# Sparse attention and a squared-ReLU expert in one kernel: batch 0 in query halves, expert chunk 0 in token halves, one-hot global rows, and casts per tile on VectorE and ScalarE

## The chip, the cores and the metric

The kernel runs on one core of one Trainium2 chip. The metric is the device time of one execution in microseconds (us), lower is better. A median is given with the number of runs behind it. Engine names: PE is TensorE, PEld its weight load, DVE is VectorE, ACT is ScalarE, POOL is GpSimd, SP is SyncE, which issues most DMA transfers here.

## The reference

Two operations follow each other. The first is attention in which a query sees a window of 32 positions on each side and 8 chosen "global" positions; global positions see and are seen by everything. The second is a two-matrix expert with a squared ReLU.

```python
# q, k, v: (8 batches, 8 heads, 576 positions, 64); global_idx: 8 sorted positions, known only at run time
scores = scale * np.matmul(q, k.transpose(0, 1, 3, 2))
mask = np.abs(pos[:, None] - pos[None, :]) <= 32
mask = mask | is_global[:, None] | is_global[None, :]
attn = softmax(np.where(mask, scores, -1e9))
x = (attn @ v) laid out as (4608 tokens, 512)
out = np.maximum(x @ w_in, 0) ** 2 @ w_out       # w_in: 512 x 2048, w_out: 2048 x 512
```

All inputs are float32; the kernel computes with 16-bit floats, so each batch of q, k and v must be cast after it is loaded.

## The kernel before

The 64 steps are (batch, head). Each step computes the scores of one head, the product with v of the head before, and four "fills" of expert work, so that TensorE always has something to do while ScalarE and VectorE handle the softmax. The expert works on 9 chunks of 512 tokens. For each chunk there are 16 "expert-in" fills (matmul with `w_in`, ReLU, square) and then 16 "expert-out" fills (matmul with `w_out`), so the work alternates between an expert-in half of four steps and an expert-out half of four steps. In the steady part, one chunk goes with one batch.

```python
def mm1(c, u):                                   # expert-in: 4 matmuls of 128x512
    ph = ps.tile([P, TC], FP32, name="ph", tag="m", bufs=3)
    ...                                          # cut: the 4 matmuls into ph
    rl = sbt("rl", [P, TC], FP16, bufs=3)
    nc.scalar.activation(out=rl, in_=ph, func=AF.Relu)
    nc.vector.tensor_tensor(out=gts[c][:, u, :], in0=rl, in1=rl, op=ALU.mult)

def tr_q(b, hp):                                 # transposes of q for two heads
    src = qnat[b % 2]
    for i in range(NT):                          # NT = 5 tiles of 120 (last: 96) positions
        nc.tensor.transpose(pt[:, ...], src[0:n, i, ts(hp, P)], identity[0:n, 0:n])
    ...                                          # cut: VectorE copies of pt into qa, qb

for s in range(B * H):
    b, h = divmod(s, H)
    n = b + 1
    if s == 1:
        ...                                      # cut: casts of batch 0, load of w_in, first fetch of batch 1
    if s == 6:
        nc.gpsimd.dma_start(out=w_out, in_=moe_w_out...)
    if h == 1 and 0 < b < B - 1:                 # next batch is cast on GpSimd, 120x2048 and 96x512 at a time
        cast(nc.gpsimd.tensor_copy, knat[n % 2], sts["k"])
        gload_kq(n)                              # 8 global rows of k and q, from a DRAM scratch
    if h == 2 and 0 < b < B - 1:
        cast(nc.gpsimd.tensor_copy, qnat[n % 2], sts["q"])
    if h == 4 and 0 < b < B - 1:
        cast(nc.gpsimd.tensor_copy, vx[n % 2], sts["v"], w=P)
        gload_v(n)
    if h == 5 and b + 2 < B and b > 0:
        fetch_next(n + 1)                        # 15 transfers, float32, into staging
    ...                                          # cut: gathers of global rows
    if s == H:                                   # expert chunk 0 runs here in one lump,
        ...                                      # cut: with the casts of batch 1 on GpSimd
    et = scores(b, h)                            # TensorE scores, ScalarE Exp -> er, VectorE mask -> et
    nb, nhp = divmod(s // 2 + 1, H // 2)
    if nb < B and s not in (H - 2, H - 1):
        (tr_q if h % 2 == 0 else tr_k)(nb, nhp)  # at h == 6 these are the NEXT batch's first q tiles
    fill(s, 2)
    if prev is not None:
        pv(*prev)                                # acc, Ln, Exp(-Ln), xT
    fill(s, 2)
    prev = (b, h, et)
```

The softmax here doesn't subtract the row's maximum and nothing guards it: scores larger than these inputs give would overflow.

## Time and profile before

The median is 402.03 us (3 runs, 398.62 to 402.93); the profiled execution spans 401.8 us at a mean granted clock of 0.983. There are three stretches.

| stretch (us) | what happens | what sets the time |
|---|---|---|
| 0 to 59.7 | loads, mask, batch 0 attention | DMA near 190 GB/s and one chain per head; no expert matmul |
| 59.7 to 117.9 | expert chunk 0 in a lump, batch 1 | mixed; loads of batch 2 and `w_out` under way |
| 117.9 to 401.8 | steady part, then a tail of expert work alone | TensorE |

Two lines of the page of before, from its part 1 (busy time of each engine and its share of the span) and part 2 (granted clock in 40 slices of the span, each about 10 us, in tenths of full speed):

```profile
PE 336.4 (84%) x2240; PEld 188.1 (47%) x2240; DVE 277.5 (69%) x603; ACT 225.3 (56%) x341; POOL 107.9 (27%) x169
PEclk9999999969979999999999999999999999999999
```

The clock is near full except for two slices in the start. The view is the chain of waits of before, in order of time (start, duration, engine and line). It shows a step at its undisturbed pace and then the one thing in each batch that disturbs it:

```profile
185.60 0.26 PE ptq L356 x5
185.86 1.73 PE po L322 x8
187.59 0.38 PE acc L403 x6
187.97 1.73 PE po L322 x8
189.70 0.38 PE sc L383 x6
...
194.83 1.74 PE ph L307 x8
196.58 0.02 issue
196.60 0.61 ACT rl L312
197.21 0.01 issue
197.22 4.70 DVE gt L313 x2
...
202.16 0.77 DVE xT L420
```

A step is 2.37 + 2.11 = 4.48 us of gapless TensorE work, so eight steps are 35.9 us. But the pattern repeats every 38.0 us (the `xT` at 164.17 comes again at 202.16). The missing 2.1 us lies in the last lines: two squares `gt` that take about 0.42 us each elsewhere take 4.70 us together. The timeline of before at that place (start, duration, engine, operation) says why:

```profile
196.60 2.44 POOL L105 CAST qnat_72<-stg 120x2048 f16<-120x2048 f32 x2
197.22 4.69 DVE L313 TENSOR_TENSOR gt<-rl 128x512 f16<-128x512 f16 x2
198.99 2.64 POOL L105 CAST vx_74<-stg 120x2048 f16<-120x2048 f32 x2
202.98 0.41 PE L403 MATMUL acc<-et,vx_73 128*128 128x160 f16 x4 [1.92 <-DVE xT L420]
```

VectorE's square stands still while GpSimd casts back to back, and TensorE is idle for 1.92 us behind it. The trace has five such places, once per batch.

The stretch table of before gives the engines' busy time in one period (columns: window, its length, then busy time of PE, PEld, DVE, ACT, POOL with instruction counts, granted clock, DMA share, GB/s):

```profile
164.17:202.16 37.99, 36.07 (x264) 20.67 (x264) 31.51 (x68) 26.20 (x41) 10.17 (x15) 1.00 0.76 124
```

### The profile page before, as it was taken

To read this page: it belongs to the slowest core of one execution; us is meant where nothing else is said; L and a number is where in the kernel's file an instruction comes from. 1 tells how busy PE (TensorE), PEld (TensorE's weight loads), DVE (VectorE), ACT (ScalarE), POOL (GpSimd) and SP (SyncE) were. 2 spreads that over 40 slices of the span, in tenths; PEclk is the share of its full clock that TensorE was granted. 3 is DMA by queue.
4 is the path that set the end of the run, shared out by engine and by line. 5 is a ranking of instruction groups with operands and counts; after the bars stand their busy time and mean duration, and the time that the engine had idled before them with its cause. 6 is when DMAs were issued, how large, how long until landed. Compare 5 with 4: busy or idle time off the path is not lost.

```text
span 401.8 us, 6380 instructions
## 1 busy us (share of the span) xinstructions
PE 336.4 (84%) x2240; PEld 188.1 (47%) x2240; DVE 277.5 (69%) x603; ACT 225.3 (56%) x341; POOL 107.9 (27%) x169
## 2 busy tenths in 40 slices
PE   0037529779768999899989989998999999999996
PEld 0025414445444555455545545554555554444442
DVE  3787636756789868986898689679867874432531
ACT  1126724634657956785597469656955982530620
POOL 5929427250048006200930180036001001000000
PEclk9999999969979999999999999999999999999999
DMA  8979998961999942991599189410001002001002
GB/s 149 192 119 190 201 194 173 197 121 62 182 198 171 186 102 82 180 160 54 121 166 153 49 164 191 90 59 34 2 33 74 1 2 78 29 8 71 28 26 78
DMA packets 126549, 43.86 MB, mean 109 GB/s; under 512 B 117110, under 2 KB 121590, under 8 KB 126518
## 3 DMA queue, kind: packets, MB, share of 16 engines
q1 hardware_dynamic: 117618, 38.29, 52.3%
q0 software_dynamic: 5904, 4.39, 7.0%
q10 hardware_dynamic: 2996, 0.79, 1.0%
q8 instruction: 17, 0.28, 0.3%
q14 instruction: 14, 0.11, 0.1%
HBM read 38.14 MB, written 9.70 MB: 119 GB/s over the span
## 4 chain that ended last, share of the span: by engine, by line
PE 72%; DVE 18%; ACT 5%; issue 2%; POOL 1%; DMA 1%; POOLq 0%; DVEq 0%
PE po L322 31%; PE ph L307 26%; DVE gt L313 6%; PE acc L403 6%; PE sc L383 5%; DVE xT L420 3%; DVE et L393 2%; PE ptq L356 2%; PE ptk L373 1%; ACT ln L415 1%; ACT ln L413 1%; ACT er L388 1%; DMA gp_100<-in_global_idx_dram 1%; ACT rl L312 1%; DVE knat_69 L105 1%
## 5 line engine op out<-in xcount | busy, mean ns | idle before, releaser
L307 PE MATMUL ph<-xT,w_in 128*128 128x512 f16 x576 | 136.2, 386 | 5.6 <-POOL xT L435 5.6
L322 PE MATMUL po<-w_out,gt 128*128 128x512 f16 x576 | 135.0, 383 | 0.0
L312 ACT ACTIVATE rl<-ph 128x512 f16<-128x512 f32 x144 | 83.7, 600 | 58.0 <-PE ph L307 44.4
L313 DVE TENSOR_TENSOR gt<-rl 128x512 f16<-128x512 f16 x144 | 81.9, 592 | 24.2 <-ACT rl L312 23.0
L307 PEld LDWEIGHTS <-w_in 128*128 128x128 f16 x576 | 55.0, 99 | 64.4 <-issue 10.1
L322 PEld LDWEIGHTS <-gt 128*128 128x128 f16 x576 | 54.4, 98 | 56.5 <-issue 1.7
L388 ACT ACTIVATE er<-sc 128x880 f16<-128x880 f32 x64 | 57.9, 905 | 31.1 <-PE sc L383 30.9
L413 ACT ACTIVATE ln<-acc 64x576 f32<-64x576 f32 x64 | 41.2, 645 | 54.6 <-PE acc L403 53.3
L435 POOL COPY xT<-gx 128x4 f16 x64 | 15.2, 238 | 203.7 <-DVE gx L431 200.2
L420 DVE TENSOR_TENSOR xT<-acc,ln 64x576 f16<-64x576 f32 x64 | 48.3, 754 | 22.5 <-ACT ln L415 22.1
L393 DVE TENSOR_TENSOR et<-er,mask 128x880 f16<-128x880 f16 x64 | 42.3, 662 | 15.0 <-ACT er L388 14.3
L415 ACT ACTIVATE ln<-ln 64x576 f32<-64x576 f32 x64 | 43.6, 681 | 2.0
L328 DVE COPY ot<-po 128x512 f32<-128x512 f32 x36 | 24.6, 685 | 24.7 <-PE po L322 24.1
L383 PEld LDWEIGHTS <-kT 128*128 128x128 f16 x384 | 30.4, 106 | 23.1 <-DVE kT L375 7.7
L373 PE MATMUL ptk<-identity,knat_69 128*128 128x128 f16 x80 | 8.4, 242 | 27.5 <-DVE knat_69 L105 19.8
L403 PE MATMUL acc<-et,vx_73 128*128 128x160 f16 (+2 forms) x192 | 20.3, 251 | 12.6 <-DVE xT L420 12.6
L416 DVE TENSOR_REDUCE gs<-acc 128x8 f32<-128x32 f32 x64 | 12.2, 191 | 21.4 <-ACT ln L413 20.1
L403 PEld LDWEIGHTS <-vx_73 128*128 128x128 f16 x192 | 15.8, 109 | 20.1 <-issue 7.8
L403 PE MATMUL acc<-et,vx_74 128*128 128x160 f16 (+2 forms) x192 | 18.0, 232 | 5.0 <-DVE xT L420 5.0
L403 PEld LDWEIGHTS <-vx_74 128*128 128x128 f16 x192 | 14.2, 100 | 12.9 <-DVE xT L420 4.8
L373 PEld LDWEIGHTS <-knat_69 128*128 128x128 f16 x80 | 5.6, 106 | 29.2 <-DVE knat_69 L105 20.0
L375 DVE COPY kT<-ptk 128x640 f16<-128x640 f16 x32 | 15.7, 489 | 1.0 <-PE ptk L373 0.4
(79 smaller groups left out, 248.4 us busy)
## 6 DMA issues: line engine op xcount, KB each, us to landing
out_dram<-ot SPq DMA_DIRECT2D x36, 256.0 KB, 2.1
stg<-in_k_dram SPq DMA_DIRECT2D x28, 240.0 KB, 5.0
stg<-in_q_dram SPq DMA_DIRECT2D x28, 240.0 KB, 11.7
stg<-in_v_dram SPq DMA_DIRECT2D x28, 240.0 KB, 6.1
w_in<-in_moe_w_in_dram POOLq DMA_DIRECT2D x4, 512.0 KB, 11.0
w_out<-in_moe_w_out_dram POOLq DMA_DIRECT2D x1, 2048.0 KB, 19.2
stg<-in_k_dram SPq DMA_DIRECT2D x7, 192.0 KB, 5.3
stg<-in_q_dram SPq DMA_DIRECT2D x7, 192.0 KB, 5.4
```

The source lines that it names most:

```text
L307: nc.tensor.matmul(ph, w_in[:, t, u * P : (u + 1) * P], xT[:, t, c * TC : (c + 1) * TC], start=(t == 0), stop=(t == NDM - 1),)
L312: nc.scalar.activation(out=rl, in_=ph, func=AF.Relu)
L313: nc.vector.tensor_tensor(out=gts[c][:, u, :], in0=rl, in1=rl, op=ALU.mult)
L322: nc.tensor.matmul(po, gts[c][:, f, m * P : (m + 1) * P], w_out[:, f, :], start=(f == 0), stop=(f == NFF - 1),)
L328: nc.vector.tensor_copy(out=ot, in_=po)
L383: nc.tensor.matmul(sc[:, bank, so : so + w], kT[:, ts(t, P)], qx[:, c0 : c0 + w], start=True, stop=True,)
L388: nc.scalar.activation(out=er.rearrange("p (b c) -> p b c", b=2), in_=sc[:, :, 0:SCW], func=AF.Exp, bias=0.0, scale=scale,)
L393: nc.vector.tensor_tensor(out=et, in0=er, in1=mask, op=ALU.mult)
L403: nc.tensor.matmul(acc[:, bank, o : o + w], vx[b % 2][:, t, v0 : v0 + P], et[:, base : base + w], start=(i % 3 == 0), stop=(i % 3 == 2), s ...
L413: nc.scalar.activation(out=ln[nr], in_=av[dr, :, :, 0:GTOK], func=AF.Ln)
L415: nc.scalar.activation(out=rec[nr], in_=ln[nr], func=AF.Exp, scale=-1.0)
L420: nc.vector.tensor_tensor(out=xT[nr, hp, b * S : (b + 1) * S].rearrange("p (b k x) -> p b k x", b=2, k=2), in0=av[nr, :, :, 0:GTOK], in1=r ...
```

## The change

The intent is to start expert work earlier and to take the casts away from GpSimd.

- Batch 0 attention runs in two query halves, and expert chunk 0 in two token halves, so that the first half chunk can start when the first queries are done.
- The 8 global rows of batch 0 are picked with one-hot matmuls instead of by an indirect DMA.
- The next batch's casts are 15 tile casts on VectorE and ScalarE, spread over heads 1 to 5. There is now a single staging set; as each tile is cast, the same tile of the batch after it is fetched.
- The global rows of batch 1 and later are fetched in float32 to the front of every staging tile, so that a tile's cast also covers them. These rows are fetched last, after all 15 tiles.
- The load of `w_out` is held back until batch 1's tiles have landed.

```diff
-    if h == 1 and 0 < b < B - 1:
-        cast(nc.gpsimd.tensor_copy, knat[n % 2], sts["k"])
-        gload_kq(n)
-    if h == 2 and 0 < b < B - 1:
-        cast(nc.gpsimd.tensor_copy, qnat[n % 2], sts["q"])
-    if h == 4 and 0 < b < B - 1:
-        cast(nc.gpsimd.tensor_copy, vx[n % 2], sts["v"], w=P)
-        gload_v(n)
-    if h == 5 and b + 2 < B and b > 0:
-        fetch_next(n + 1)
...
+def cast_batch(n, t):
+    cast_tile(nc.vector.tensor_copy, "k", n, t)
+    cast_tile(nc.scalar.copy, "q", n, t)
+    cast_tile(nc.vector.tensor_copy if t % 2 else nc.scalar.copy, "v", n, t)
...
+for h in range(H):                              # batch 0, first query half
+    et = scores(0, h, (0,))
+    ...                                         # cut: casts, transposes, v globals per pair of heads
+    if h == 5:
+        for nm in "kqv":
+            for t in range(NT):
+                fetch(nc.sync, nm, 1, t)
+        fetch_globals(1)
+    ...                                         # cut: memsets for batch 1, prev, step
+for h in range(H):                              # batch 0, second query half
+    et = scores(0, h, (1,))
+    fill(step, 1); pv(*prev); fill(step, 1)
+    ...                                         # cut: prev, step
+    if h == 1:
+        nc.gpsimd.tensor_copy(out=w_out[0:1, 0, 0:1], in_=st["v"][32:33, 4, 511:512])   # holds w_out back
+        for i in range(4):
+            nc.gpsimd.dma_start(out=w_out[:, ts(i, 4), :], in_=wo[:, ts(i, 4), :])
+    if h >= 5:
+        for t in ((0,), (1, 2), (3, 4))[h - 5]:
+            cast_batch(1, t)
...
+for b in range(1, B):
+    n = b + 1
+    plan = {3: (0, 1), 4: (2, 3), 5: (4,)} if b == 1 else {t + 1: (t,) for t in range(NT)}
+    for h in range(H):
+        if b == 1 and h == 0:
+            ...                                 # cut: fetch of all tiles of batch 2
+            fetch_globals(n)
+        et = scores(b, h, (0, 1))
+        nb, nhp = divmod(b * NHP + h // 2 + 1, NHP)
+        if nb < B:
+            (tr_q if h % 2 == 0 else tr_k)(nb, nhp)
+        fill(step, 2)
+        if prev is not None: pv(*prev)
+        fill(step, 2)
+        prev = (b, h, (0, 1), et)
+        for t in plan.get(h, ()) if n < B else ():
+            cast_batch(n, t)
+            if n + 1 < B:
+                for nm in "kqv":
+                    fetch(nc.sync, nm, n + 1, t)
+        ...                                     # cut: gathers of global rows
+        if h == 7 and n + 1 < B:
+            fetch_globals(n + 1)
```

`tr_q` now transposes its five tiles in reverse order, `for i in reversed(range(NT))`, so the first of them needs the tile that is cast last.

## The prediction

> **What bounds it now.** The page gives 401.8 us, TensorE 84% busy. The chain of waits has three stretches.
> (1) 0 to 59.7 us: no expert matmul. The first `et` is at 28.9 us: the mask waits for indices by DMA and a GpSimd memset. Then each head of batch 0 costs 3.1 us: accumulate 0.91, Ln 0.66, Exp 0.69, `xT` 0.77; one `acc`, so nothing overlaps. DMA runs near 190 GB/s.
> (2) 59.7 to 116.5 us: chunk 0 runs in one lump while GpSimd casts batch 1; four later steps hold only attention (about 3.3 us each).
> (3) From 116.5 us: TensorE bound. The chain repeats every 38.0 us per batch. An unhindered step is 2.37 + 2.11 = 4.48 us, 35.9 per batch; the other 2.1 us is one stall: in the timeline at 197.2 us two `gt` products take 4.69 us (median 0.425 each) while GpSimd casts `qnat` and `vx` (1.9 us each). The Trainium skill, "SBUF — State Buffer", section "SBUF: two separate sides", says VectorE and GpSimd share a port pair as an exclusive lock; this trace agrees. Five such stalls remain. The tail from 335.6 us is pure matmul at 0.216 us each and doesn't change.
>
> **Change.** Removed: GpSimd casts with their stalls (5 x 2.1 = 10 us); the index wait; the single `acc` of batch 0; the attention-only steps (chunk 0 is spread over the second half and batch 1). Added: one-hot matmuls, two evacuations per pair; per batch 8 ScalarE casts (about 0.6 us, interpolated between the traced 0.40 at 256 and 1.04 at 1024 elements) and 7 VectorE casts (about 0.6).
>
> *Steady part.* In the expert-in half ScalarE already fills 4.35 of 4.48 us per step (0.90+0.64+0.68+4x0.54), VectorE about 4.0. Casts at heads 1 to 5 land there and add about 3 us to each; buffers should hide most. I expect stalls of 1 us per batch instead of 2.1: gain 5 us.
>
> *Start.* First scores near 18 us, first half about 3 us per step (casts, transposes and copies in the same queues), ending near 43; expert matmuls from 47. But loads bind: batch 0 is issued until about 26 us, `w_in` takes about 13, batch 1 about 19, so batch 1 lands near 59; `w_out` and batch 2 near 90. In-order casts on ScalarE and VectorE wait for whole batches plus globals, which GpSimd used to absorb: about 5 us near 54 to 59, some 8 us at batch 1, head 3. So batch 2, head 2 (116.5 us before) comes at 110 to 121. Batch 2 can be fetched only after batch 1 is cast: one staging set. The early expert work is mostly given back to loads.
>
> Sum: 402 - 5 (steady) - 2 (start) = **395 us, range 379 to 409**. Chances: faster by over 2% 0.45, within 2% 0.47, slower 0.08.
>
> **What would show it.**
> - First expert matmul between 44 and 50 us, half width; first `et` by 20 us.
> - No `gt` above 1 us in the steady part; batch period 36.5 to 37.5 us.
> - Casts waiting for staging DMA in the second half of batch 0 and at batch 1 heads 3 to 5; TensorE idle there.
> - ScalarE near full in the expert-in half; `ph` waiting for ReLU or `acc` for `xT` about 1 us per batch.
> - Batch 2, head 2 within 5 us of 116.5.
>
> **What would make it wrong.** If batches 1 and 2 land before their casts are reached, the start gains 15 to 20 us and the time is 375 to 380. If casts stall TensorE 2 to 4 us per batch, the steady gain vanishes and it is 400 or more.

## The result, and the profile after

The median after is 426.69 us (5 runs, 424.65 to 429.4), against 402.03 us before (5 runs on the same chip, 398.4 to 402.93). The ratio is 1.0636, with a 95% interval of 1.0565 to 1.0707: slower. Here and below, a ratio is the mean time of one kernel's fast runs over that of the other's of the same rounds, so it isn't quite the ratio of the medians quoted. The range of the prediction (379 to 409) did not hold the result.

The same two lines of the page, after:

```profile
PE 350.9 (82%) x2402; PEld 203.1 (48%) x2402; DVE 268.9 (63%) x711; ACT 264.9 (62%) x453; POOL 45.8 (11%) x124
PEclk9999965785999989998999999899989999999999
```

GpSimd is relieved (107.9 to 45.8 us) and ScalarE took over (225.3 to 264.9). The clock line has new dips: a broad one in slices 6 to 10, and then single 8s, of which some are four slices apart, which is one batch.

A convenient mark is the first expert matmul at head 2 of a batch, where the steady pattern begins. Spans are those of the profiled executions. The profiled run of after is the slowest of its five (429.4 us, median 426.69), so a difference of up to 3 us between its profile and another run's can be that alone.

| mark | before (us) | after (us) | difference |
|---|---|---|---|
| first expert matmul | 59.7 | 44.2 | -15.5 |
| batch 2, head 2 | 117.9 | 131.0 | +13.1 |
| batch 6, head 2 | 270.8 | 293.6 | +22.8 |
| end of the span | 401.8 | 427.3 | +25.5 |

So the start loses 13.1 us although it begins 15.5 us earlier, and from there on the steady part loses the remaining 12.4.

**The steady part.** The chain of waits after reaches the mark at 171.71, 212.36, 252.99 and 293.63 us: a period of 40.65 us. The stretch table for one period, and for that of the next period cut into four:

```profile
171.71:212.36 40.65, 38.23 (x266) 21.28 (x264) 29.98 (x76) 30.16 (x49) 2.00 (x8) 0.96 0.64 120
...
212.36:230.81 18.45, 18.12 (x127) 9.99 (x125) 15.84 (x42) 17.81 (x31) 0.00 (x0) 1.00 0.85 148
230.81:233.34 2.53, 0.44 (x6) 0.39 (x7) 1.84 (x4) 2.51 (x6) 0.00 (x0) 1.00 1.08 186
233.34:237.10 3.76, 3.76 (x16) 1.82 (x14) 1.61 (x5) 0.83 (x2) 0.00 (x0) 0.55 0.93 166
237.10:253.00 15.90, 15.90 (x119) 9.27 (x118) 10.69 (x25) 9.01 (x13) 2.00 (x8) 1.00 0.25 66
```

In the first part, the expert-in half, ScalarE is busy for 17.81 of 18.45 us: ReLUs, softmax and casts fill its queue. In the second part TensorE does almost nothing and the clock is still 1.00. In the third, TensorE works without a pause, but at a granted clock of 0.55 on average: it is 0.50 for 3.41 us of it, from 233.62 to 237.03 us. In the last part everything is back to normal and ScalarE has time to spare (9.01 of 15.90). The timeline of TensorE after, then that of ScalarE, across that gap (in brackets: the idle time before, and what ended it):

```profile
230.26 0.55 PE L451 MATMUL sc<-qa_80,kT 128*128 128x160 f16 x6
232.90 0.45 PE L390 MATMUL tr<-identity,qnat_71 104*128 104x104 f16 x5 [2.09 <-ACT qnat_71 L309]
233.18 3.18 PE L345 MATMUL mm<-w_out,gt 128*128 128x512 f16 x8
```

```profile
228.77 1.08 ACT L333 ACTIVATE rl<-mm 128x512 f16<-128x512 f32 x2
...
231.25 1.09 ACT L333 ACTIVATE rl<-mm 128x512 f16<-128x512 f32 x2
232.22 0.62 ACT L309 CAST qnat_71<-stq 104x512 f16<-104x512 f32 x1
```

TensorE reaches head 6 and finds that the last q tile of the next batch isn't cast. The cast is at the end of a ScalarE queue that has never paused. As the transposes go in reverse order, all five wait, and with them the expert-out matmuls that are ready behind them. After the gap the first group of eight expert-out matmuls takes 3.18 us by the timeline, where the same group takes 1.89 us later. The five slow `gt` squares of before are gone: the longest `gt` of after takes 0.43 us.

**The start.** The waits of TensorE after, from 40 to 110 us (in all, how often, the longest), then those of ScalarE from 50 to 108 us:

```profile
PE mm L328 <- ACT rl L333: 14.2, 3, 13.1
PE acc L478 <- DVE et L466: 12.7, 2, 10.5
PE mm L328 <- POOL xT L521: 7.0, 2, 3.6
```

```profile
ACT qnat_70 L309 <- DMA stq<-gscr_q_362: 11.5, 1, 11.5
ACT qnat_71 L309 <- DMA stq<-gscr_q_301: 9.0, 1, 9.0
```

The third line of the first fence is GpSimd's copy of global columns into `xT`; it belongs to the halves themselves (a run without these loads, e6 below, has the same 7.0 us). The first two lines hold two long gaps of TensorE, of 10.45 us up to 64.6 us and of 13.06 us up to 104.5 us. In each, ScalarE and VectorE stand before the first cast of a batch and wait for the transfer named `gscr`: the global rows, fetched behind all 15 tiles of the batch. The first cast of batch 1 could start at 61.6 us, that of batch 2 at 101.1 us, and the first q casts 0.6 to 0.9 us later. In the stretch table the granted clock is 0.50 from 56.1 to 80.0 us, although TensorE works again from 64.6 us, with pauses.

### The profile page after: what moved, and what is told of

It is laid out like the page before. It is cut to its first block, busy times and chain, and to the rows that moved or that the text cites. A ratio compares the mean times of both kernels' runs of the same rounds, so it can differ in the third digit from the quotient of the medians.

```text
span 427.3 us, 6931 instructions
## 1 busy us (share of the span) xinstructions
PE 350.9 (82%) x2402; PEld 203.1 (48%) x2402; DVE 268.9 (63%) x711; ACT 264.9 (62%) x453; POOL 45.8 (11%) x124
## 4 chain that ended last, share of the span: by engine, by line
PE 53%; ACT 15%; issue 12%; DVE 4%; SPq 2%; DMA 1%; POOL 1%; ACTq 0%; POOLq 0%
PE mm L345 30%; PE mm L328 14%; ACT rl L333 6%; PE acc L478 3%; PE sc L451 3%; ACT er L465 3%; ACT ln L490 2%; PE tr L390 2%; DMA stq<-gscr_q_362 1%; SPq L121 1%; ACT qnat_70 L309 1%; DVE et L466 1%; ACT qnat_71 L309 1%; PE tr L415 1%; POOL w_out L597 1%
## 5 line engine op out<-in xcount | busy, mean ns | idle before, releaser
L328 PE MATMUL mm<-xT,w_in 128*128 128x512 f16 (+1 forms) x640 | 143.8, 367 | 22.9 <-ACT rl L333 15.9
L345 PE MATMUL mm<-w_out,gt 128*128 128x512 f16 x576 | 140.5, 394 | 0.0
L333 ACT ACTIVATE rl<-mm 128x512 f16<-128x512 f32 (+1 forms) x160 | 83.8, 554 | 40.6 <-PE mm L328 38.6
L465 ACT ACTIVATE er<-sc 128x880 f16<-128x880 f32 (+2 forms) x72 | 59.4, 825 | 21.6 <-PE sc L451 21.2
L334 DVE TENSOR_TENSOR gt<-rl 128x512 f16<-128x512 f16 (+1 forms) x160 | 59.4, 394 | 20.3 <-ACT rl L333 15.8
L490 ACT ACTIVATE ln<-acc 64x576 f32<-64x576 f32 (+1 forms) x72 | 42.6, 592 | 46.5 <-PE acc L478 45.4
L498 DVE TENSOR_TENSOR xT<-acc,ln 64x576 f16<-64x576 f32 (+1 forms) x72 | 49.6, 689 | 30.1 <-ACT ln L491 27.1
L466 DVE TENSOR_TENSOR et<-er,mask 128x880 f16<-128x880 f16 (+2 forms) x72 | 40.5, 562 | 29.1 <-ACT er L465 26.3
L491 ACT ACTIVATE ln<-ln 64x576 f32<-64x576 f32 (+1 forms) x72 | 45.2, 628 | 2.3
L351 DVE COPY ot<-mm 128x512 f32<-128x512 f32 x36 | 24.7, 685 | 24.9 <-PE mm L345 24.4
```

Source lines behind the costliest of these rows:

```text
L328: nc.tensor.matmul(ph, w_in[:, t, u * P : (u + 1) * P], xT[:, t, c * TC + a : c * TC + z], start=(t == 0), stop=(t == NDM - 1),)
L333: nc.scalar.activation(out=rl[:, 0 : z - a], in_=ph, func=AF.Relu)
L334: nc.vector.tensor_tensor(out=gts[c][:, u, a:z], in0=rl[:, 0 : z - a], in1=rl[:, 0 : z - a], op=ALU.mult)
L345: nc.tensor.matmul(po, gts[c][:, f, m * P : (m + 1) * P], w_out[:, f, :], start=(f == 0), stop=(f == NFF - 1),)
L465: nc.scalar.activation(out=ev, in_=sv, func=AF.Exp, bias=0.0, scale=scale)
L466: nc.vector.tensor_tensor(out=tv, in0=ev, in1=mv, op=ALU.mult)
```

## The experiments

All ran beside the kernel before on the same chip; its median in those rounds was 400.46 to 401.59 us. Each experiment has 4 runs. "Head 2" means the first expert matmul of batch 2, head 2 (after: 131.0 us), and "period" the repeat of the steady pattern (after: 40.65 us).

| run | change | median us | ratio to before (95%) | head 2 | period |
|---|---|---|---|---|---|
| e1_pool_casts | after, casts on GpSimd | 412.56 | 1.0264 (1.0204 to 1.0325) | 131.1 | 36.16 |
| e2_late_tr | after, transposes of head 6 later | 411.16 | 1.0270 (1.0238 to 1.0302) | 128.6 | 37.43 |
| e3_casts_out_half | after, casts at heads 0, 1 | 412.22 | 1.0296 (1.0263 to 1.0329) | 131.7 | 36.44 |
| e4_no_load2 | after, batch 2 not loaded (wrong result) | 418.70 | 1.0451 (1.0401 to 1.0500) | 121.9 | 40.6, once 39.0 |
| e5_wout_early | after, `w_out` not held back | 429.89 | 1.0686 (1.0642 to 1.0731) | 135.0 | 40.6, once 39.0 |
| e6_no_load12 | after, batches 1 and 2 not loaded (wrong result) | 407.78 | 1.0129 (1.0075 to 1.0183) | 112.0 | 40.6 |
| e7_before_casts_out | before, tile casts at heads 0, 1 | 396.24 | 0.9861 (0.9799 to 0.9923) | | 36.73 |
| e8_before_casts_in | before, tile casts at heads 1 to 5 | 443.34 | none (two of four runs slow) | | about 47 |
| e8b_before_casts_in | the same, fetches per tile | 405.43 | 1.0124 (1.0072 to 1.0177) | | 38.69 |
| e9_dummy_mm | after, the gap filled with dummy matmuls | 422.47 | 1.0527 (1.0477 to 1.0576) | 134.3 | 38.94 |
| e10_casts_lump | after, casts of batches 1, 2 in one lump | 425.27 | 1.0593 (1.0540 to 1.0646) | about 127.5 | |
| e11_lump_out_late | e10, e3 and e2 together | 409.32 | 1.0191 (1.0135 to 1.0247) | 129.9 | 36.44 |
| e12_globals_mid | after, global rows fetched between k and q | 422.78 | 1.0547 (1.0508 to 1.0585) | 123.4 | |
| e13_no_wout | after, `w_out` not loaded (wrong result) | 421.47 | 1.0509 (1.0463 to 1.0555) | 123.7 | |

My first theory had two parts. For the steady part: the casts stand in the expert-in half, where ScalarE is full, and the wait of head 6's transposes for the last q cast, with the clock drop that follows, is the loss. The rival was that the extra work on ScalarE and VectorE costs the time wherever it stands. For the start: batches 1 and 2 land later than predicted, and the casts wait for them. The rival was that in-order casts on ScalarE and VectorE block the softmax, which GpSimd used to avoid.

### e1_pool_casts: the same casts on GpSimd

```diff
 def cast_batch(n, t):
-    cast_tile(nc.vector.tensor_copy, "k", n, t)
-    cast_tile(nc.scalar.copy, "q", n, t)
-    cast_tile(nc.vector.tensor_copy if t % 2 else nc.scalar.copy, "v", n, t)
+    cast_tile(nc.gpsimd.tensor_copy, "k", n, t)
+    cast_tile(nc.gpsimd.tensor_copy, "q", n, t)
+    cast_tile(nc.gpsimd.tensor_copy, "v", n, t)
```

> The changed kernel, with all casts of batches 1 to 7 given back to GpSimd, each at the same place. Theory (two causes: casts that sit in the in-order queues of VectorE and ScalarE while the loads are late, costing about 10 us at the start; and ScalarE overfull in the expert-in half, about 2.65 us per batch against before): batch period back to about 38.0 us with gt stalls again, the two TensorE gaps near 54 to 64 and 92 to 104 us shortened or moved, time about 405 to 412 us against 427. Rival (the halved start and the one staging set cost the time, wherever the casts run): start unchanged, only the period changes, time 416 to 420.

Measured: 412.56 us; the period fell to 36.16 us and head 2 stayed at 131.1. In the steady part I expected the old period of 38.0 us with its stalls; what came is the shortest period of any run. The casts stay in the expert-in half: at batch 4 they run from 208.6 to 218.5 us, and the expert-in half begins at 209.7. So the amount of work that was taken off ScalarE and VectorE, and the queue in which the last q cast stands, changed together in this run; e2 and e3 tell them apart. For the start it speaks for the loads: with VectorE and ScalarE free of casts, TensorE still waited 11.97 us in one piece, up to 110.8 us, now for a q cast on GpSimd, and head 2 came no sooner.

The run shows the stall of before once more, in the timeline of VectorE at 143 us, but only in the first of its five steady batches (that one took 42.5 us). The second line is what the squares beside casts take in the other four:

```profile
142.88 5.92 DVE L334 TENSOR_TENSOR gt<-rl 128x512 f16<-128x512 f16 x2
...
284.82 1.56 DVE L334 TENSOR_TENSOR gt<-rl 128x512 f16<-128x512 f16 x2
```

The timeline of GpSimd at the first of the two places:

```profile
143.13 0.62 POOL L309 CAST knat<-stk 128x512 f16<-128x512 f32 x1
...
147.59 0.60 POOL L306 CAST vx<-stv 104x512 f16<-104x512 f32 x1
```

At 143 us, one square took 5.59 us while nine casts of 0.6 us ran back to back. In the other four batches (from 172, 208, 244 and 281 us on) squares and casts alternated: a cast took 0.6 to 1.0 us, a square 0.81 to 0.86 us instead of 0.42, and TensorE did not wait for it. Why the two got into step four times and not the fifth is open. The kernel before, with nothing changed but the size of its GpSimd casts, was not run.

### e2_late_tr: the transposes of head 6 behind two expert fills

```diff
-            if nb < B:
+            if nb < B and h != 6:
                 (tr_q if h % 2 == 0 else tr_k)(nb, nhp)
             fill(step, 2)
+            if nb < B and h == 6:
+                tr_q(nb, nhp)
```

> The changed kernel, but at head 6 of each batch the q transposes of the next batch come after the first two fills instead of before them. Theory (TensorE waits 2.1 us for the last q cast, which stands at the end of a late ScalarE queue, and its clock is then halved for about 3 us): the wait shrinks to under 0.5 us, no half clock there, batch period from 40.65 to about 37, time about 410 to 414. Rival (ScalarE work itself is what is too much per batch, the wait only shows it): the wait moves to ph or acc, period stays above 39.5, time 422 or more.

Measured: 411.16 us, a period of 37.43 us, as expected. The wait shrank to 0.36 us and the clock stayed at 1.00 in the whole period. Every cast is still there, on the same engine at the same place, so the wait at head 6 and what follows it make up 3.2 us of the period.

### e3_casts_out_half: the same casts on the same engines, at heads 0 and 1

```diff
         plan = {3: (0, 1), 4: (2, 3), 5: (4,)} if b == 1 else {t + 1: (t,) for t in range(NT)}
+        if b >= 3:
+            plan = {0: (0, 1, 2), 1: (3, 4)}
...
-            if h == 7 and n + 1 < B:
+            if h == (7 if b == 1 else 6 if b == 2 else 4) and n + 1 < B:
                 fetch_globals(n + 1)
```

> The changed kernel, but from batch 3 on the casts come at heads 0 and 1 (the expert-out half, where ScalarE is half idle) instead of heads 1 to 5; globals fetched earlier to suit. Same work on the same engines. Theory (the place of the casts, not their amount, makes the steady loss): period of batches 3 to 6 falls from 40.65 to 36 to 36.5 us, below the 38.0 of before; time about 409 to 412. Rival (the amount of cast work on ScalarE and VectorE makes it): period stays at 40, time 424 or more.

Measured: 412.22 us; the period from batch 3 on is 36.44 us, as expected. The stretch table of one period:

```profile
207.54:243.98 36.44, 36.12 (x265) 20.74 (x264) 29.92 (x76) 30.12 (x49) 2.29 (x8) 1.00 0.83 134
```

VectorE and ScalarE are as busy as in after (29.92 and 30.12 us, against 29.98 and 30.16) with the same number of instructions, yet the period is 4.2 us shorter. This fells the rival for the steady part: the amount of work isn't the cost, its place is.

### e9_dummy_mm: the gap filled, so that the clock doesn't drop

```diff
+            if nb < B and h == 6 and b >= 2:
+                dm0 = mm_bank()
+                for _ in range(10):
+                    nc.tensor.matmul(dm0, w_in[:, 0, 0:P], xT[:, 0, 0:512], start=True, stop=True)
             if nb < B:
                 (tr_q if h % 2 == 0 else tr_k)(nb, nhp)
```

> The changed kernel with ten idle 512-column matmuls (2.16 us, result unused) put before the q transposes at head 6 of batches 2 to 6, where TensorE otherwise stands 2.1 us. The wait is filled, not shortened. Theory (the halved clock after the wait is a cost of its own, about 2 us per batch, caused by the gap): no half clock there, period from 40.65 to 38.3 to 38.9, time about 417 to 420. Rival (the clock drop has another cause or costs nothing beyond the wait): period 40 or more, time within 3 us of 427.

Measured: a period of 38.94 us, 1.7 us less than after, with a clock of 1.00 throughout. The timeline of TensorE in this run, at the place of the gap:

```profile
230.49 2.32 PE L624 MATMUL mm<-xT,w_in 128*128 128x512 f16 x10
232.74 0.45 PE L390 MATMUL tr<-identity,qnat 104*128 104x104 f16 x5
233.02 1.89 PE L345 MATMUL mm<-w_out,gt 128*128 128x512 f16 x8
```

The transposes come no earlier, but the group after them is at full speed. So the wait costs 2.1 us and the clock another 1.7. e4 (below) happens to confirm this with nothing filled in: its code at head 6 is that of after, and its waits there are 2.09 us long in all five batches, but in one batch the clock stayed full. The stretch table of e4 for that period and for the next:

```profile
162.40:201.40 39.00, 36.58 (x269) 20.83 (x266) 30.01 (x76) 30.18 (x49) 2.00 (x8) 1.00 0.66 125
201.40:242.00 40.60, 38.18 (x268) 21.36 (x266) 29.93 (x76) 30.12 (x49) 2.00 (x8) 0.96 0.64 120
```

The total of e9, 422.47 us, missed the 417 to 420 expected, because the start of this run came out 3.3 us later (head 2 at 134.3, with a first gap of 12.53 us); the edit doesn't touch the start, and why that gap varies by 2 us stays open.

With these runs the period of after adds up: 36.44 (casts in the other half, e3) + 2.09 (wait) + 1.71 (clock, e9) + 0.33 (TensorE waits for ReLUs, 1.3 us over four periods) = 40.57, of 40.65 measured.

### e7_before_casts_out: the cast part alone, in the better half

This is the kernel before, with nothing of the new start. From batch 3 on its casts are tile casts on VectorE and ScalarE at heads 0 and 1, and the fetches come earlier.

```diff
-        if h == 1 and 0 < b < B - 1:
+        if h == 1 and 0 < b < 3:
             cast(nc.gpsimd.tensor_copy, knat[n % 2], sts["k"])
             gload_kq(n)
...                                                 # the same for q at h == 2 and v at h == 4
-        if h == 5 and b + 2 < B and b > 0:
+        if b + 2 < B and h == (5 if b == 1 else 2) and b not in (0, 2):
             fetch_next(n + 1)
...                                                 # b == 2: k, q, v fetched at heads 2, 3, 5
         prev = (b, h, et)
+        if 3 <= b < B - 1 and h < 2:
+            ...                                     # cast_tile per tile: k on VectorE, q on ScalarE, v on both
+            if h == 1:
+                gload_kq(n)
+                gload_v(n)
```

> The kernel before, start untouched; from batch 3 on its casts leave GpSimd and run per tile on VectorE and ScalarE at heads 0 and 1, in the expert-out half; loads moved earlier to suit. Theory: no port stall and no ScalarE overload, so the period falls from 38.0 to about 36.4 for batches 3 to 6: 5 to 7 us less than before, 394 to 396. Rival (the casts cost VectorE and ScalarE as much as they save): within 2 us of before.

Measured: 396.24 us (394.61 to 398.79), ratio 0.9861 with an interval of 0.9799 to 0.9923. It is the only version that beats both kernels. The period is 36.73 us against 38.0, and only batches 3 to 6 have it. The gain of 1.4% is clear of 1, but the interval doesn't decide whether it passes 2%.

### e8_before_casts_in and e8b_before_casts_in: the cast part alone, in the change's half

```diff
-        if h == 1 and 0 < b < B - 1:
+        if h == 1 and b == 1:
             cast(nc.gpsimd.tensor_copy, knat[n % 2], sts["k"])
             gload_kq(n)
...                                                 # the same for q and v
+        if 2 <= b < B - 1 and 1 <= h <= NT:
+            cast_tile(n, h - 1)
+            if b + 2 < B:                           # e8b only; e8 fetched all 15 tiles at head 6
+                for nm, src in (("k", k), ("q", q), ("v", v)):
+                    fetch_tile(nc.sync, src, n + 1, sts[nm], h - 1)
+            if h == 1:
+                gload_kq(n)
+                gload_v(n)
```

> The kernel before, start untouched; from batch 2 on its casts run per tile on VectorE and ScalarE at heads 1 to 5, where the change puts them: this part of the change alone. Theory: the wait for the last q cast at head 6, and a period of 40 to 40.7 instead of 38.0 us for batches 2 to 6; 10 to 14 us more than before, 412 to 416. Rival (the loss belongs to other parts of the change): period 38 or less, within 3 us of before.

e8 was confounded and tells little: 443.34 us with a period of about 47, but its 15 fetches at head 6 stood in SyncE's queue ahead of the output stores. VectorE waited 29.9 us in all, in four pieces, for output buffers. Again, with the fetches spread per tile:

> As e8 (the kernel before, casts of batches 3 to 7 per tile on VectorE and ScalarE at heads 1 to 5, this part of the change alone), but with the fetches issued tile by tile after the casts as the change does; in e8 they stood as a block of 15 ahead of the output stores, which made the output copies wait 29.9 us in all, so e8's time says nothing about casts. Theory: wait of about 2 us for the last q cast at head 6 and a period of 39 to 40.7 instead of 38.0 for batches 2 to 6: 407 to 416. Rival (the steady loss belongs to other parts of the change): period 38 or less, 399 to 403.

Measured: 405.43 us, a period of 38.69 us, less than I expected. So this part of the change, by itself, costs about 1.2%. The TensorE timeline of e8b at head 6:

```profile
212.61 0.38 PE L374 MATMUL ptq<-identity,qnat 120*128 120x120 f16 x4
214.85 0.22 PE L374 MATMUL ptq<-identity,qnat 104*128 104x104 f16 x1 [1.86 <-ACT qnat L123]
214.90 1.89 PE L340 MATMUL po<-w_out,gt 128*128 128x512 f16 x8
```

The wait is there, almost as long as in after (1.86 us, five times), but the group behind it runs at full speed: 1.89 us. In before's order four of the five transposes run ahead of the wait and only the last one stands behind it. In after, the reversed order puts all five behind. The missing clock drop (1.7 us in e9) is most of the difference between 38.69 and 40.65 us: without it the wait costs about what the old VectorE stall did. That the order of the transposes is what spared the clock is not shown: after was never run with the forward order.

### e4_no_load2 and e6_no_load12: without the loads

These two leave out the loads of batch 2, and of batches 1 and 2, and cast whatever is in the staging set. The result is wrong.

```diff
             if b == 1 and h == 0:
-                for nm in "kqv":
-                    for t in range(NT):
-                        fetch(nc.sync, nm, n, t)
-                fetch_globals(n)
+                pass                                # e6 does the same for batch 1
```

> Wrong results on purpose: batch 2 is not fetched, its casts read the staged data of batch 1 once more, so nothing waits for that load. Theory (the second gap, 13 us near 92 to 104 us, is the wait of in-order casts for batch 2, fetched late since one staging set is freed only by the casts of batch 1): the gap vanishes, batch 2 head 2 comes 11 to 15 us sooner, time about 412 to 415. Rival (the start is limited by engine work, the loads only look late): under 5 us gained.

> Wrong results on purpose: neither batch 1 nor batch 2 is fetched, both are cast from the staged data of batch 0, so no cast of the start waits for a load; all instructions of the engines are as in the changed kernel. Theory (the start is lost to loads alone): the gap of 10.8 us near 54 to 65 us goes too, with the half clock after it, and batch 2 head 2 comes near 106 to 112 us, sooner than the 117.9 of the kernel before; time 402 to 408 with the steady period still 40.6. Rival (the two-half order of batch 0 is itself slow): head 2 no sooner than 118.

Measured: head 2 at 121.9 us without batch 2 (9.1 us earlier) and at 112.0 us without both (9.9 us earlier again). So waiting for the loads costs 19 us of the start, and without that the halves would reach head 2 about 6 us before the old kernel's 117.9. The halves do gain time, though less than I had counted on (see below); the loads eat it and more. With its 13.06 us gap gone, e4 should have reached 412 to 415 us; it took 418.70, a miss of about 4. The first gap remained, at 10.8 us. e6 is still 1.3% slower than before, because its period is 40.6.

### e5_wout_early: `w_out` not held back

```diff
-            nc.gpsimd.tensor_copy(out=w_out[0:1, 0, 0:1], in_=st["v"][32:33, 4, 511:512])
             for i in range(4):
                 nc.gpsimd.dma_start(out=w_out[:, ts(i, 4), :], in_=wo[:, ts(i, 4), :])
```

> The changed kernel without the one-element copy that holds the load of w_out back until batch 1 has landed (62 us); it now goes out at about 42 us, together with batch 1. The steady part is as in the changed kernel (period 40.6). Theory (the transfer engines stand partly idle near 57 to 64 us because w_out and batch 2 both wait for batch 1; the sum of bytes up to batch 2 is what counts): batch 1 lands later, near 67 us, batch 2 sooner, near 90 instead of 101, and batch 2 head 2 comes near 121 to 125 instead of 131; time about 417 to 421. Rival (later batch 1 costs as much as earlier batch 2 gives): start and time within 3 us of the changed kernel.

Measured: 429.89 us, not faster than after (3.2 us more by the medians, about 2 by the ratios to before); the theory failed, and its rival held or nearly so. The first gap doubled to 21.28 us (batch 1 shared the DMA engines with `w_out` and landed near 74 us), the second shrank to 5.03 us. And from 70 to 80 us the DMA share was only 0.27: with a single staging set, batch 2 can't be fetched until batch 1 is cast.

### e10_casts_lump and e11_lump_out_late: the casts of batches 1 and 2 in one lump

The theory: if tile casts spread over several heads free the staging tiles late, casting them all in one place should help, and keep the softmax from waiting behind them.

```diff
-        if h >= 5:
-            for t in ((0,), (1, 2), (3, 4))[h - 5]:
+        if h == 7:
+            for t in range(NT):
                 cast_batch(1, t)
...
-        plan = {3: (0, 1), 4: (2, 3), 5: (4,)} if b == 1 else {t + 1: (t,) for t in range(NT)}
+        plan = {5: (0, 1, 2, 3, 4)} if b == 1 else {t + 1: (t,) for t in range(NT)}
```

> The changed kernel with the casts of batch 1 all at head 7 of the second half (instead of heads 5 to 7), and those of batch 2 all at head 5 (instead of heads 3 to 5). Nothing in between then stands behind a cast whose load has not landed, and the staging set is freed in about 5 us instead of 9.5. Theory (spread casts block the queues and delay the fetch of batch 2): batch 2 head 2 at 117 to 123 us instead of 131, time about 413 to 420. Rival (only the landing of the loads counts, wherever the casts stand, as the run with casts on GpSimd suggests): head 2 within 4 us of 131.

> The changed kernel with three repairs together: lumped casts as in e10, casts of batch 3 on at heads 0 and 1 as in e3, q transposes at head 6 after two fills as in e2. Theory: the gains add, start about 10 us and steady about 18 us: 397 to 404, level with the kernel before, not under e7 (396.2). Rival: they overlap, 408 or more.

Measured: e10 425.27 us, head 2 at about 127.5, not the 117 to 123 expected. The gaps moved and stayed: 5.75 us up to 64.4, and 12.88 us up to 106.2, the latter at the transposes of batch 2. Taking the casts out of the softmax's way changes where TensorE waits, not when the data is there. e11 put this together with e2 and e3: the steady part is as good as in e3 (36.44), but the start gained little (129.9), and 409.32 us misses the 397 to 404 expected.

### e12_globals_mid and e13_no_wout: what makes the loads late

What was still open was why batch 1 and batch 2 landed later than predicted: because of the global rows at the end of each batch's queue, or because `w_out` takes its share of the DMA engines?

```diff
-            for nm in "kqv":                        # e12, for batch 1 and again for batch 2
+            for t in range(NT):
+                fetch(nc.sync, "k", 1, t)
+            fetch_globals(1)
+            for nm in "qv":
                 for t in range(NT):
                     fetch(nc.sync, nm, 1, t)
-            fetch_globals(1)
```

```diff
-            nc.gpsimd.tensor_copy(out=w_out[0:1, 0, 0:1], in_=st["v"][32:33, 4, 511:512])    # e13
-            for i in range(4):
-                nc.gpsimd.dma_start(out=w_out[:, ts(i, 4), :], in_=wo[:, ts(i, 4), :])
+            nc.gpsimd.memset(w_out, 0.0)
```

> The changed kernel with the global rows of batches 1 and 2 fetched between the k and the q tiles instead of last. In the changed kernel the casts wait for the global rows (issued at 55.7, landed at 61.6 us) while the transfer engines are only 0.26 to 0.3 busy from 60 to 64 us. Theory (that tail is in series with each batch): the first gap of TensorE ends 2 to 3 us sooner (62 instead of 64.6), the second as well, batch 2 head 2 at 125 to 128 instead of 131, time 421 to 424. Rival (the tile loads themselves land that late): head 2 within 1.5 us of 131, time within 2 us of 427.

> Wrong results on purpose: w_out is filled with zeros by GpSimd instead of being loaded, all else as in the changed kernel. Theory (from 62 us on w_out and batch 2 share the transfer engines, and w_out takes about 13 us of them): the wait for batch 2 at its casts shrinks from 13 us to under 2, batch 2 head 2 at 119 to 123 instead of 131, time 415 to 419. Rival (batch 2 is late because its tiles are issued late behind the casts of batch 1): the wait stays above 6 us, head 2 later than 126.

The waits of TensorE from 40 to 125 us, in e12 and then in e13 (whose result is wrong):

```profile
PE mm L328 <- ACT rl L333: 9.8, 3, 9.1
PE acc L478 <- DVE et L466: 9.0, 4, 5.9
```

```profile
PE acc L478 <- DVE et L466: 14.2, 4, 11.1
...
PE mm L328 <- ACT rl L333: 5.5, 3, 5.1
```

e12: the order of three small transfers alone brings head 2 from 131.0 to 123.4 us, more than I expected. Both gaps shrink by about 4 us: to 5.9, ending at 60.5, and to 9.1, ending at 97.0. The time, 422.78, is inside what I expected; by the medians the gain over after is 3.9 us, not 7.6, as the profiled run of after is 2.7 us above its median and the first steady period of e12 is 1.1 us longer than that of after. A batch's first cast waits for its global rows; when they are last of 18 transfers, the whole batch waits for the last transfer.

e13: head 2 comes at 123.7, 7.3 us earlier (by the medians, 5.2 us are gained), as the second gap shrinks to 5.1. A gap of 5.1 us lies between the two figures of the expectation (under 2, over 6), and the time is above 415 to 419, so neither account holds alone: with e12 I count both causes as real. (The first gap of e13 is 11.12 us, so what it gains is in the second.) What is left of batch 2's lateness isn't bandwidth: in e13 the DMA share was only 0.23 from 60 to 65 us and 0.42 from 65 to 70, while fetches waited for staging tiles to be cast. How the 19 us divide among the three (rows last, `w_out`, one staging set) isn't settled: they overlap, and no run takes the staging set's part away alone.

## Why the prediction was wrong

**The steady part was predicted at -5 us and came out at about +12.** The bottleneck was read correctly: TensorE bound, a period of 38.0 us with one 2.1 us stall, and that stall did go away with the GpSimd casts (the longest `gt` in after is 0.43 us). The load on ScalarE in the expert-in half was also right. The step that failed is this: "Casts at heads 1 to 5 land there and add about 3 us to each; buffers should hide most. I expect stalls of 1 us per batch instead of 2.1". (The "each" of that sentence are ScalarE and VectorE.) The term was 4.2 us (40.57 to 36.44 above; e3), not 1:

- The place was not foreseen. I looked for the stall at `ph` waiting for a ReLU or at `acc` waiting for `xT`, where buffers lie between the engines. There the waits were indeed small (0.33 us per period). The stall is at the transposes of head 6, which need the last cast itself. No buffer lies between these two. e2 shows it: the same casts, and the transposes behind two expert fills (1.7 us), and 3.2 us are gone.
- The clock was not foreseen. After the wait of 2.09 us the next 3.41 us run at half clock, which costs another 1.7 us (e9, and the one spared batch of e4). The skill, "TensorE: Matmul & The Clock Gate", section "What's actually happening", states that the clock falls to half after an idle window of about 3.4 us and comes back after a busy one. The trace agrees on the two speeds and, here, on the length of the slow stretch (3.41 us at 0.50), but not on the gap that it takes: TensorE stood still for 2.09 us, and 2.37 us passed between the last score matmul and the first expert-out matmul (230.81 to 233.18), the transposes included. The page's section "Part 4: PE-mode transpose" says that transposes don't count as busy in the same way; no run here tests that. e8b, with waits of 1.86 us (2.13 with the transposes, 212.77 to 214.90), and before, with 1.91 to 1.99 us, kept the full clock. But the length of the gap alone doesn't decide: in e4 (181.02 to 183.11 us) and in e5 (194.12 to 196.21 us) one gap of the same 2.09 us, with the same work around it, left the clock at 1.00, while the other four of each run halved it. In all sixteen traces the clock changes only at multiples of 3.41 us from its other changes, and the two spared gaps began 0.11 and 0.12 us before such a multiple (one in after that began 0.04 us before it was not spared). So where the gap falls on that beat matters too; a threshold can't be read from these runs.

The prediction did say that stalls of 2 to 4 us per batch would make it 400 or more, and that is what came, a little worse.

**The start was predicted at -2 us (head 2 at 110 to 121) and came out at +13 (131.0).** What was right: first `et` by 20 us (15.3), the first expert matmul between 44 and 50 us (44.2), the casts of a batch waiting in ScalarE and VectorE for the whole batch plus globals, and the place of both gaps. Two sizes failed. The first is the loads: "batch 1 lands near 59; `w_out` and batch 2 near 90", with waits of "about 5 us near 54 to 59, some 8 us at batch 1, head 3". They landed at 61.6 and about 101.1, and the gaps of TensorE were 10.45 and 13.06 us, where 13 were predicted for both; taking the loads away brought head 2 forward by 19 us (e6). The second is the work of the engines: "If batches 1 and 2 land before their casts are reached, the start gains 15 to 20 us". e6 has no such waits, and its head 2 is at 112.0, a gain of 6 us. So of the miss against the middle of the predicted range (131.0 against 115.5) about 6 us are the loads (19 against 13) and 9.5 are not, by an estimate from these figures. In e6 TensorE waits 7.0 us for GpSimd's copies of global columns into `xT`, and its clock is 0.50 from 60.9 to 71.2 us; the prediction has neither, and how the 9.5 us divide is open. The landing time was wrong because I added up bytes at the traced rate, and left out three things that put them in series:

- The global rows come last in the queue, and the first cast needs them (e12: 7.6 us of head 2 in the profiles, 3.9 us of the median).
- `w_out` is started at 62.0 us, when batch 1 has landed, and so shares the DMA engines with batch 2 (e13: 7.3 us of head 2, 5.2 us of the median).
- Batch 2 is fetched tile by tile as batch 1 is cast, and those casts start only when batch 1 is complete. I had written that down ("one staging set"), but not charged for the DMA engines' idle time: a share of 0.43 from 60 to 65 us in after.

On top came the half clock from 56.1 to 80.0 us with the first gap, and a short one after the second. I did not measure its part in the start by itself.

**In-order casts blocking the softmax**, which the prediction named as well, is not the main thing: with GpSimd doing the casts (e1), or with casts in one lump (e10), TensorE waits elsewhere for the same data.

**Of the signs to look for**, "no `gt` above 1 us" and the first matmul held; the batch period (36.5 to 37.5) and head 2 within 5 us of 116.5 did not. The tail of pure expert matmul did not change, as predicted.

## What to carry to other kernels

When work is moved to another engine, ask not only whether that engine has time on average (ScalarE was at 62%), but whether it has time in the stretch where the work is put, and who consumes the last piece of it: the same casts cost 4.7 us per batch in one half of the period and 0.5 in the other (40.65 and 36.44 against an undisturbed 35.9), and moved to the better half alone they made the old kernel 1.4% faster (e7). A consumer that stands in front of other ready work in an in-order queue should stand as late as it can, since a TensorE gap can be paid for again at half clock. Nor was another engine the only way out of the stall that the change set out to remove: with GpSimd casting one tile at a time (e1) the period was 36.16 us, and the stall came in one batch of five. And in a load plan, look at what the first consumer waits for: three small transfers queued behind fifteen large ones held back a whole batch.

## What the Trainium skill lacked or had wrong

- "TensorE: Matmul & The Clock Gate", sections "What's actually happening" and "HAM oscillation — how this bites in real kernels": the working rule there is no idle gap above about 3.4 us. Here a gap of 2.09 us dropped the granted clock to 0.50 for 3.41 us in every batch of after, at a cost of 1.7 us, while the same gap left it alone in one of five batches of e4 and of e5, and gaps of 1.86 to 1.99 us (e8b, before) never dropped it. A note that gaps of about 2 us can suffice would have helped.
- The same page gives the time to recover as one busy window. In the start the clock stayed at 0.50 from 56.1 to 80.0 us. TensorE was back at 64.6 us, but busy for only 1.86 of 5 us (65 to 70) and 1.05 of 5 us (70 to 75), and the clock came back after 5 us of continuous work. The page has no number for work as sparse as this.
- "SBUF — State Buffer", section "SBUF: two separate sides", describes the lock between VectorE and GpSimd as held for the whole instruction. The traces agree that VectorE is blocked, but show it blocked across a run of instructions: in before, in all five batches, one square of about 3.9 us over three GpSimd casts (1.89, 0.61 and 1.89 us), and in e1 once, one of 5.59 us over nine casts of 0.6 us, although that square is on record as started 0.25 us before the first of them. In the other four batches of e1 the two alternated (squares of 0.81 to 0.86 us). So short GpSimd instructions helped in four batches of five, and the page doesn't tell when they do.
